# Softmax row sums on VectorE with one adding transfer, weight sums spread over the units, and a transposition moved behind the third scores

## The chip, the cores and the metric

One core of one Trainium2 chip runs the whole program. The metric is the device time of one execution in microseconds (us). Kernels are compared only within the same rounds. Names of engines: PE is TensorE, DVE is VectorE, ACT is ScalarE, POOL is GpSimd.

## The reference, cut to what matters

```python
# attention: q, k, v of shape (4, 8, 768, 64); six hash bits per row
mask = q_bucket[:, :, :, None] == k_bucket[:, :, None, :]
scores = scale * np.matmul(q, k.transpose(0, 1, 3, 2))
scores = np.where(mask, scores, -1000000000.0)
attn = np.exp(scores - np.max(scores, axis=-1, keepdims=True))
attn = attn / (np.sum(attn, axis=-1, keepdims=True) + 1e-09)
x = np.matmul(attn, v)                    # then (B,H,S,D) -> (B*S, H*D)
# feed-forward with a PReLU between two products
h = x @ w_in
g = np.maximum(h, 0.0) + alpha * np.minimum(h, 0.0)
return g @ w_out
```

## The kernel before

The attention stage works through 32 units: 16 pairs of heads, and for each the two halves of the queries. In a unit PE makes six score tiles in three groups of two ("first", "second" and "third scores"), ACT makes exponentials of them (`pt`), and one unit later PE multiplies these with v (`attend`) and with a matrix of ones (`totals`). Between these PE turns (transposes) q and k of the next pair in the even units and hashes them in the odd ones. DVE and GpSimd add six exponential tiles into one per unit. DVE also rounds one piece of the feed-forward's weights per unit (`weight_parts`, `weight_sum`), makes sums of rounded weights (`weight_group`; the products are of a kind with seven multiplications in place of eight, which needs such sums) and divides. The same kind of product needs four such sums (here differences) of the attention's result x for each batch; they are called the x sums, and GpSimd makes those of the first batch during the attention stage. After the attention stage come the products.

The loop of a unit, as it was:

```python
scores(u, 0)
add_first(u)                       # POOL: tile 0 + tile 1
...
if u > 0:
    add_last(u - 1)                # DVE: tiles 3 + 4, + 5, + POOL's sum
# (turn or hash of the first half), attend(u - 1, 0)
weight_parts(u)
scores(u, 1)
add_third(u)                       # POOL: + tile 2
weight_sum(u)
weight_group(u)                    # DVE: four sums at once, every 4th unit, later every 2nd
if more:
    if g == 0:
        turn(pi + 1, "k", 0)       # PSUM slot of the tag "mi"
        turn(pi + 1, "k", 1)       # the other one
    else:
        hash_bits(pi + 1, 1)
if u > 0:
    attend(u - 1, 1)
    totals(u - 1)                  # PSUM slot of the tag "mi"
...
scores(u, 2)
if u > 0:
    divide(u - 1)                  # DVE: its first step reads the totals
...
if u == HW:                        # HW = 16: w_in is rounded, the first batch's x long complete
    load_w(0); load_w(1); load_x(0); sums_x(0)     # the x sums: four subtractions on POOL
```

PSUM is the memory into which PE writes its results. The tag "mi" has two PSUM slots, taken in turn by both halves of a turn, by a hash and by the totals. Whoever takes a slot waits until the tile two takings back has been read.

## Time and profile before

| | before |
|---|---|
| median of 4 runs | 998.84 us (997.56 to 999.87) |
| span of the profiled run | 998.3 us |
| the add of 128x768, mean of 32, on DVE | 1667 ns |
| GpSimd: two adds per unit, mean of the first | 1939 ns |

```profile
PEclk9999999998999999999999999999999999999999
...
L676 DVE TENSOR_TENSOR accd<-accd,accp 128x768 f32<-128x768 f32 x32 | 53.4, 1667 | 3.3
```

These are two lines of the page: the granted clock of PE in 40 slices of the span, and a group of instructions with its busy time in us, the mean ns of one, and the idle time of its engine before it. The tenth slice (about 225 to 250 us) is the only one below 9. The mean of 1667 ns for the third add of DVE lies between the two durations that the prediction shows for it, 0.96 us with GpSimd idle and 2.39 us beside a GpSimd add.

### The profile page before, as it was taken

What the parts mean: (1) busy time and instruction counts of PE and PEld (TensorE: products, weight loads), DVE (VectorE), ACT (ScalarE), POOL (GpSimd) and SP (SyncE); (2) the same over time, 40 slices, a digit from 0 to 9 for tenths busy, and PEclk for the clock granted to TensorE, in tenths of its full rate; (3) what the DMA queues carried; (4) which work ended last, traced back from release to release, by engine and by line L of the source; (5) the groups of instructions that cost most, each with busy time, mean ns of one, the idle gap of its engine ahead of it and who ended that gap; (6) DMA issues with size and microseconds to landing.
All of it is one profiled execution on the core that took longest, in us unless ns stands there. A gap on an engine that the chain in (4) does not pass through costs nothing.

```text
span 998.3 us, 12489 instructions
## 1 busy us (share of the span) xinstructions
PE 963.2 (96%) x4741; PEld 594.0 (60%) x4741; DVE 605.8 (61%) x959; ACT 371.0 (37%) x669; POOL 158.5 (16%) x98
## 2 busy tenths in 40 slices
PE   6999999989999998999999999999999999999997
PEld 3444444434444443455788655888656888556886
DVE  3999999999999999766600366500467300665100
ACT  6777676665777664222100122100222000222000
POOL 2333333262333333000300000300000300000000
PEclk9999999998999999999999999999999999999999
DMA  7465756355444431463400133300224200231000
GB/s 199 126 182 143 237 154 179 107 164 157 143 143 143 127 111 53 200 259 110 137 22 22 58 111 99 123 22 21 71 88 155 68 22 22 84 111 37 22 22 24
DMA packets 93316, 106.81 MB, mean 107 GB/s; under 512 B 53296, under 2 KB 79936, under 8 KB 93248
## 3 DMA queue, kind: packets, MB, share of 16 engines
q1 hardware_dynamic: 91680, 105.54, 33.1%
q8 instruction: 39, 0.64, 0.3%
q10 hardware_dynamic: 1568, 0.39, 0.2%
q14 instruction: 29, 0.24, 0.1%
HBM read 78.65 MB, written 27.26 MB: 106 GB/s over the span
## 4 chain that ended last, share of the span: by engine, by line
PE 61%; DVE 35%; ACT 1%; issue 1%; DMA 1%; DVEq 0%; SPq 0%; ACTq 0%
PE z_2a L756 6%; PE z_1a L756 6%; PE z_0a L756 6%; DVE accd L676 5%; DVE accd L675 4%; DVE accd L674 4%; DVE wx L553 3%; PE z_1c L756 3%; PE z_0c L756 3%; PE z_2c L756 3%; DVE wr L577 2%; DVE wr L557 2%; PE f_2a L756 2%; PE f_3a L756 2%; PE f_7a L756 2%; PE f_6a L756 2%
## 5 line engine op out<-in xcount | busy, mean ns | idle before, releaser
L658 ACT ACTIVATE pt<-sc 128x768 f32<-128x768 f32 x192 | 149.9, 813 | 119.8 <-PE sc L653 119.8
L653 PE MATMUL sc<-qT,kT 64*128 64x384 f32 x768 | 157.5, 487 | 0.0
L686 PE MATMUL av<-pt,vn 128*64 128x385 f32 (+1 forms) x768 | 138.1, 495 | 0.0
L667 POOL TENSOR_TENSOR accp<-pt,pt 128x768 f32<-128x768 f32 x32 | 62.0, 1939 | 222.5 <-ACT pt L658 185.2
L686 PEld LDWEIGHTS av<-pt,vn 128*64 128x64 f32 x768 | 49.4, 136 | 72.6 <-issue 72.6
L732 POOL TENSOR_TENSOR x<-x,x 128x768 f32<-128x768 f32 x16 | 31.9, 2005 | 364.0 <-DMA x<-x_s 363.4
L810 DVE TENSOR_TENSOR g<-g,g 128x384 f32<-128x384 f32 x128 | 82.5, 665 | 2.2
L653 PEld LDWEIGHTS sc<-qT,kT 64*128 64x128 f32 x768 | 69.8, 190 | 15.3 <-issue 15.2
L653 PEld LDWEIGHTS <-kb 64*128 64x128 bf16 x384 | 24.4, 94 | 79.3 <-issue 62.7
L653 PE MATMUL sc<-qb,kb 64*128 64x384 bf16 x384 | 64.6, 329 | 5.6 <-ACT pt L658 5.6
L670 POOL TENSOR_TENSOR accp<-accp,pt 128x768 f32<-128x768 f32 x32 | 62.3, 1946 | 39.0 <-ACT pt L658 38.9
L756 PE MATMUL z_2a<-wo,g 128*128 128x256 f32 x256 | 58.0, 379 | 0.5 <-ACT z_2u L763 0.5
L756 PE MATMUL z_1a<-wo,g 128*128 128x256 f32 x256 | 57.9, 379 | 0.0
L756 PE MATMUL z_0a<-wo,g 128*128 128x256 f32 x256 | 57.9, 379 | 0.0
L676 DVE TENSOR_TENSOR accd<-accd,accp 128x768 f32<-128x768 f32 x32 | 53.4, 1667 | 3.3
L803 DVE SCALAR_TENSOR_TENSOR g<-h,alpha 128x384 f32<-128x384 f32 x32 | 22.1, 692 | 54.4 <-ACT h L795 54.4
L756 PEld LDWEIGHTS z_2a<-wo,g 128*128 128x128 f32 x256 | 48.6, 190 | 8.1 <-ACT z_2u L763 0.9
L756 PEld LDWEIGHTS z_0a<-wo,g 128*128 128x128 f32 x256 | 48.6, 190 | 7.5
L756 PEld LDWEIGHTS z_1a<-wo,g 128*128 128x128 f32 x256 | 48.6, 190 | 6.6
L675 DVE TENSOR_TENSOR accd<-accd,pt 128x768 f32<-128x768 f32 x32 | 43.7, 1364 | 3.3
L674 DVE TENSOR_TENSOR accd<-pt,pt 128x768 f32<-128x768 f32 x32 | 40.3, 1260 | 0.0
L639 ACT ACTIVATE qb<-hs,hb 32x384 bf16<-32x384 f32 x64 | 36.7, 574 | 2.2 <-PE hs L636 1.0
(217 smaller groups left out, 1477.1 us busy)
## 6 DMA issues: line engine op xcount, KB each, us to landing
wi<-w_in_s SPq DMA_DIRECT2D x32, 896.0 KB, 4.6
raw<-in_moe_w_in_dram SPq DMA_DIRECT2D x16, 512.0 KB, 4.1
raw<-in_moe_w_out_dram SPq DMA_DIRECT2D x16, 512.0 KB, 3.6
w_in_s<-wsi SPq DMA_DIRECT2D x16, 448.0 KB, 5.4
w_out_s<-wso SPq DMA_DIRECT2D x8, 896.0 KB, 4.4
wo<-w_out_s SPq DMA_DIRECT2D x8, 896.0 KB, 7.4
qn<-in_q_dram SPq DMA_DIRECT2D x32, 192.0 KB, 3.7
vn<-in_v_dram SPq DMA_DIRECT2D x16, 384.0 KB, 4.4
```

The lines of the kernel that those rows point to most:

```text
L639: do(ACT.activation(bits["q", pi][D * s : D * s + 32, cols], ps[r], AF.Sign, bias=hb[r]))
L653: do(PE.matmul(sc[:, s, :CW], what["k", pi][r, ks], what["q", pi][r, qs], start=first, stop=not first,))
L658: do(ACT.activation(pt[:, :, :CW], sc[:, :, :CW], AF.Exp, scale=SCALE / DOWN))
L667: do(POOL.tensor_tensor(accp[u], p(u, 0), p(u, 1), op=ALU.add))
L670: do(POOL.tensor_tensor(accp[u], accp[u], p(u, 2), op=ALU.add))
L674: do(DVE.tensor_tensor(accd[u], p(u, 3), p(u, 4), op=ALU.add))
L675: do(DVE.tensor_tensor(accd[u], accd[u], p(u, 5), op=ALU.add))
L676: do(DVE.tensor_tensor(accd[u], accd[u], accp[u], op=ALU.add))
L686: do(PE.matmul(av[u][D * s : D * s + D, :w], nat["v", pi][:, s, kc * D : (kc + 1) * D], prob[u, kc][:, s, :w], start=(kc == 0), stop=(kc = ...
L732: do(POOL.tensor_tensor(x_m[b, to], x_m[b, a], x_m[b, c], op=ALU.subtract))
L756: do(PE.matmul(self.ps[bank], self.left(left, k), self.right(right, k), start=start and k == 0, stop=k == self.nk - 1, skip_group_check=no ...
L810: do(DVE.tensor_tensor(g_m[to, i], g_m[x, i], g_m[y, i], op=op))
```

## The change

The intent: GpSimd's adds slow DVE down, so they go. DVE makes the first add itself, and the third tile is added by a transfer. The weight sums, four at once, made single units long for DVE; they are now queued and made one or two per unit. And the second turn (or hash) moves behind the third scores, so that PE has work while ACT makes exponentials.

```diff
+    def weight_sums(count):
+        while sums_due and (count or sums_due[0][0].__name__ == "store"):
+            ...                                    # [cut: one queued sum, or the store]
     def add_first(u):
-        do(POOL.tensor_tensor(accp[u], p(u, 0), p(u, 1), op=ALU.add))
+        do(DVE.tensor_tensor(accp[u], p(u, 0), p(u, 1), op=ALU.add))
     def add_third(u):
-        do(POOL.tensor_tensor(accp[u], accp[u], p(u, 2), op=ALU.add))
+        nc.gpsimd.dma_start(accp[u], p(u, 2), accum_op=ALU.add)
@@ the loop of a unit
         scores(u, 0)
-        add_first(u)
         if u > 0:
             add_last(u - 1)                        # now without the add of accp
+        add_first(u)
+        if u > 0:
+            add_total(u - 1)                       # the add of accp
@@
         weight_sum(u)
+        weight_sums(1 if u < HW else 2)
         weight_group(u)                            # now only queues
-        if more: ...                               # second turn or hash
         attend(u - 1, 1); totals(u - 1)
         scores(u, 2)
         divide(u - 1)
+        if more: ...                               # second turn or hash
-        if u == HW:
+        if u == HW + 2:
             load_w(0); load_w(1); load_x(0); sums_x(0)
```

More of the change, by code (lines that the diff above doesn't have):

```diff
@@ L584, in weight_sum @@
         ))
+    sums_due = []
     def weight_group(i):
@@ L597, in weight_group, with one, store @@
             return
-        for to, a, c in sums4:
+        def one(to, a, c):
             do(DVE.tensor_tensor(w[:, to], w[:, a], w[:, c], op=ALU.subtract))
-        if i < HW:
-            c, kk = divmod(n, 2)
-            for ii in range(4):
-                nc.sync.dma_start(w_in_s[4 * c + ii][:, :, kk], w[:, :, ii])
-        else:
-            nc.sync.dma_start(w_out_s[n], w)
+        def store():
+            if i < HW:
+                c, kk = divmod(n, 2)
+                for ii in range(4):
+                    nc.sync.dma_start(w_in_s[4 * c + ii][:, :, kk], w[:, :, ii])
+            else:
+                nc.sync.dma_start(w_out_s[n], w)
+        for x in sums4:
+            sums_due.append((one, x))
+        sums_due.append((store, ()))
+    def weight_sums(count):
+        while sums_due and (count or sums_due[0][0].__name__ == "store"):
+            fn, x = sums_due.pop(0)
+            count -= fn.__name__ == "one"
+            fn(*x)
     def turn(pi, name, half):
@@ L675, in add_last, with add_total @@
         do(DVE.tensor_tensor(accd[u], accd[u], p(u, 5), op=ALU.add))
+    def add_total(u):
         do(DVE.tensor_tensor(accd[u], accd[u], accp[u], op=ALU.add))
@@ L893, in fast_path @@
         weight_sum(u)
+        weight_sums(1 if u < HW else 2)
         weight_group(u)
-        if more:
-            if g == 0:
-                turn(pi + 1, "k", 0)
-                turn(pi + 1, "k", 1)
-            else:
-                hash_bits(pi + 1, 1)
         if u > 0:
@@ L908, in fast_path @@
             divide(u - 1)
+        if more:
+            if g == 0:
+                turn(pi + 1, "k", 0)
+                turn(pi + 1, "k", 1)
+            else:
+                hash_bits(pi + 1, 1)
         load_weight(u + 3)
-        if u == HW:
+        if u == HW + 2:
             load_w(0)
@@ L928, in fast_path @@
     add_last(last)
+    add_total(last)
     attend(last, 1)
@@ L932, in fast_path @@
     divide(last)
+    weight_sums(4)
     attn.close()
```

## The prediction

> **What bounds the kernel now.** I read the page's first two parts, then the table of stretches, then the timeline of the attention stage engine by engine, and only then the chain of waits.
>
> ```profile
> PE 963.2 (96%) x4741; PEld 594.0 (60%) x4741; DVE 605.8 (61%) x959; ACT 371.0 (37%) x669; POOL 158.5 (16%) x98
> ...
> 75.00:125.00 50.00, 48.75 (x330) 21.36 (x328) 47.79 (x70) 35.75 (x60) 16.76 (x9) 1.00 0.64 190
> 175.00:225.00 50.00, 46.18 (x308) 20.32 (x306) 47.96 (x61) 33.84 (x56) 23.44 (x12) 1.00 0.48 137
> 225.00:275.00 50.00, 48.49 (x306) 21.63 (x308) 47.65 (x72) 32.77 (x55) 14.79 (x8) 0.93 0.49 149
> 600.00:700.00 100.00, 100.00 (x419) 79.20 (x418) 31.80 (x51) 13.85 (x32) 7.89 (x4) 1.00 0.20 66
> ```
>
> The columns of the stretches are PE, weight loads, DVE, ACT, POOL, granted clock, DMA share, GB/s. After about 410 us (the matrix products) PE is full, and the change does not touch that. The attention stage, about 15 to 410 us, has 32 units (16 head pairs, two query halves); only there can time go. Both PE and DVE are over 95% busy in it, so the averages do not say which one binds.
>
> ```profile
> 130.53 0.87 PE L614 MATMUL tp_q<-ident,qn 128*128 128x128 f32 x6
> 130.58 0.95 DVE L674 TENSOR_TENSOR accd<-pt,pt 128x768 f32<-128x768 f32 x1
> 131.34 2.16 PE L686 MATMUL av<-pt,vn 128*64 128x384 f32 x12
> 132.43 1.85 POOL L667 TENSOR_TENSOR accp<-pt,pt 128x768 f32<-128x768 f32 x1 [6.98 <-ACT pt L658]
> 132.70 2.39 DVE L676 TENSOR_TENSOR accd<-accd,accp 128x768 f32<-128x768 f32 x1
> 135.14 0.87 PE L614 MATMUL tp_k<-ident,kn 128*128 128x128 f32 x6
> 135.72 1.71 DVE L553 TENSOR_SCALAR wx<-wx 128x512 uint32<-128x512 uint32 x1
> 137.93 0.82 PE L698 MATMUL sm<-accd,ones 128*64 128x384 f32 x4
> ...
> 142.36 0.51 PE L636 MATMUL hs<-kT,wh 128*32 128x384 f32 x1
> 142.67 1.50 ACT L658 ACTIVATE pt<-sc 128x768 f32<-128x768 f32 x2
> ```
>
> From the starts on PE, a unit is the same run of stages each time: first turn (or hash) 0.80, weighted sum of v 2.09, second scores 1.72, second turn 0.80, weighted sum 1.98, totals 0.75, then third scores and the next unit's first scores together 3.68. Sum 11.82 us. Most units are exactly that, whatever DVE does: PE has little left to give. It loses a little (1) where four score tiles follow one another (3.68 against 2 x 1.72 = 3.44: they wait for the exponentials, 0.24 per unit); (2) after a unit with weight sums, where the next turn waits for DVE to read the totals (a turn takes 1.61 in place of 0.80); (3) once, when GpSimd makes the x sums; (4) in the last two units, which have no turns, and where DVE is slower than PE (12.5 and 11.7 us).
>
> ```profile
> 210.37 8.39 POOL L732 TENSOR_TENSOR x<-x,x 128x768 f32<-128x768 f32 x4
> 212.68 2.19 DVE L557 SCALAR_TENSOR_TENSOR wr<-raw,wr 128x512 f32<-128x512 uint32 x1
> 224.74 0.96 DVE L676 TENSOR_TENSOR accd<-accd,accp 128x768 f32<-128x768 f32 x1
> 226.34 0.43 DVE L553 TENSOR_SCALAR wx<-wx 128x512 uint32<-128x512 uint32 x1
> ```
>
> This is the key to DVE: the same instructions with GpSimd idle. The add is 0.96 where it is 2.39 above, the shift 0.43 where it is 1.71.
>
> ```profile
> PE 61%; DVE 35%; ACT 1%; issue 1%; DMA 1%; DVEq 0%; SPq 0%; ACTq 0%
> ```
>
> The chain of waits runs through DVE for the whole attention stage. I take that with care: DVE never rests there, so a chain traced back through it finds no gap, yet PE's stages are as tight.
>
> **What the Trainium skill says.** "SBUF — State Buffer", section "Who interferes with whom": VectorE's second port pair is shared with GpSimd and locked for a whole instruction; a VectorE instruction with two SBUF inputs, or in a two-port mode, blocks against a GpSimd one that reads SBUF. The trace agrees (2.39 against 0.96; 1.71 against 0.43). "DMA: Bandwidth & Descriptors", section "SWDGE vs HWDGE vs iDMA": an accumulating transfer can only be issued from GpSimd, which writes its descriptors in software into SBUF. No transfer of that kind is in this trace. The same page, "Anatomy of one DMA — SWDGE (gpsimd) path", fits 2.0 us plus bytes over 436 GB/s, which is 2.9 us for 393 KB; the trace's plain 384 KB load of v takes 4.4, which I use. "Trainium Kernel Development and Optimization", section "Performance Expectations", warns that matmul busy time is a bad metric; hence the stage starts above instead of 96%.
>
> **The change part by part.**
>
> *DVE, per unit.* Removed: blocking by GpSimd, (2.39 - 0.96) + (1.71 - 0.43) = 2.7 us in the unit shown. Added: one 128x768 add, about 0.9 from start to start. Weight sums: before four at once (4 x 0.69 = 2.8 us every fourth unit, later 4 x 0.43 = 1.7 every second), now one (0.69) or two (0.86) per unit, the same total. Uncontended DVE per unit, start to start: adds 1.06 + 0.87 + 0.90 + 0.87 = 3.7; weight rounding 0.73 + 0.46 + 0.46 + 0.73 + 0.72 + 0.71 = 3.8; division 0.61 + 0.20 + 0.26 + 0.61 + 0.53 = 2.2; sums 0.7 to 0.9; together 10.4 to 10.6. That is about 1 us under PE's unit, so DVE's throughput stops binding.
>
> *PE, per unit.* The second turn or hash now stands between third and next first scores. It removes the 0.24 wait: 3 x 1.72 + 2 x 0.80 + 2.09 + 1.98 + 0.75 = 11.58 us.
>
> *The new wait.* The moved turn of k comes right after the totals in the small PSUM pair, so its second half takes the bank of the totals: it must wait until DVE has read them, the first step of the division. Let T be the end of third scores. The last exponential ends at T + 1.0 (142.36 shows hashes starting 1.7 after 140.6; ACT trails by 0.9). If the unit had a hash, ACT now does its three signs first (1.75), then the weight's absolute value and the square (1.4), and the next two exponentials (1.5): T + 5.6. DVE's first add needs both of them. After it: two adds 1.8, rounding 3.8, one sum 0.65, the transpose that reads the totals 0.57, so T + 12.4. PE wants the bank at T + 11.58 + 0.40 = T + 12.0. It stalls 0.5 us in every second unit, 0.75 with two sums.
>
> *Sum.* First half: a pair of units took 24.03 (48.04 us for four, first to fifth add of that kind), now 2 x 11.58 + 0.5 = 23.66; 8 pairs give 3.0. Second half: 24.39 now 23.91; 6 pairs give 2.9. Last units: traced the same way, the first product step after the totals starts about 29.4 us after unit 29's third scores, before 33.3 (409.58 - 376.32); 3.9 less. The x sums: four GpSimd adds of 2.1 us still block DVE, two units later, for about 6 us, and PE stalls as before: 0. The late sums of the last group (4 x 0.45) fall where PE has work queued: 0. Total 9.8 us: 999.6 - 9.8, about 990 us.
>
> **The rivals.**
> (a) *The adding transfer becomes the wait.* It can be issued at about T + 7.2 (its tile's exponential), and the adding of the totals needs it at about T + 17.7: 10.5 us of room. The v load takes 4.4; an accumulate must read its destination too, so I estimate 6 to 8 with descriptors. For: DMA is already half busy in this stage, and DVE's two-port steps may hold up descriptors. Against: the room. If it took 12 or 13 us, each unit would lose 1 to 3 us: 1020 to 1080.
> (b) *PE loses all stalls.* If ACT and DVE run slightly earlier than I work out, the 0.5 to 0.75 stall is gone: 8 x 0.87 + 6 x 1.23 + 3.9 = 18 us, 981; without the x sums' stall also, 976.
> (c) *DVE was the real bound, as the chain says.* Then a unit would go from 12.38 to about 10.6: 55 us saved, 945. PE's 11.82 in nearly every unit speaks against it.
> (d) *ACT's order costs more.* The exponentials now come 2 us later; if score tiles wait for them, PE gains nothing: about 1000.
>
> **Range and chances.** The gain is bounded by PE's tight stages at some 20 us, and the estimate sits in the middle; the transfer is the one unknown that could cost much. 990, with 979 to 1002 for 8 in 10. Faster by over 2% means under 979.6: only rival (b) in full, 0.11. Slower by over 2% (above 1019.6) only by rival (a): 0.07. Within: 0.82.
>
> **What would show it.** Right: the adds on DVE at 0.95 to 0.97 and the shift at 0.43 in all units but the one with x sums; the chain of waits moving from DVE to PE in the attention stage; units of 11.6 and 12.1 in turn on PE; a wait of the k turn on the transpose of the division; DVE waiting for the exponentials before the first add. Wrong: waits of the total add on a DMA (rival a), a DVE still long in its adds although GpSimd is idle (descriptors on the same ports), score tiles waiting on ACT (d), or no k-turn wait at all (b).

## The result, and the profile after

The changed kernel took 993.76 us in the median (4 runs, 993.52 to 995.21) against 998.84. The ratio is 0.9953, with a 95% interval from 0.9936 to 0.997: faster, but by less than 2%. Here and below a ratio is the mean time of one kernel's fast runs over that of the other's fast runs of the same rounds, so it is not quite the ratio of the medians.

The page of the changed kernel (its engine rows, PE's granted clock, the shares in the chain of waits, three groups of instructions, and the adding transfer with KB and median us from issue to landing):

```profile
PE 959.8 (97%) x4741; PEld 590.5 (60%) x4741; DVE 557.9 (56%) x991; ACT 373.1 (38%) x669; POOL 72.5 (7%) x66
PEclk9999999997999999999999999999999999999999
...
PE 77%; DVE 10%; ACT 8%; issue 3%; DMA 1%; SPq 0%; ACTq 0%; DVEq 0%
...
L685 POOL DMA_DIRECT2D accp<-pt x32 | 38.5, 1204 | 344.6 <-DVE accd L693 145.8
L682 DVE TENSOR_TENSOR accp<-pt,pt 128x768 f32<-128x768 f32 x32 | 30.7, 958 | 46.8 <-ACT pt L673 46.8
L693 DVE TENSOR_TENSOR accd<-accd,accp 128x768 f32<-128x768 f32 x32 | 30.5, 953 | 1.9 <-DMA accp<-pt 1.8
...
accp<-pt POOLq DMA_DIRECT2D x32, 384.0 KB, 4.8
```

DVE took on 32 more instructions and is busy 48 us less (557.9 for 605.8). The same add that took 1667 ns in the mean takes 953. The chain of waits went from DVE to PE, as foreseen. The transfer lands in 4.8 us and was waited for only 1.8 us in all. But the tenth slice of the clock went from 8 to 7: the x sums cost more than before.

One even unit of the changed kernel, cut to the lines that count (start, duration, engine, line of the kernel, operation, tiles; in brackets the idle time before and what ended it):

```profile
132.83 0.96 DVE L682 TENSOR_TENSOR accp<-pt,pt 128x768 f32<-128x768 f32 x1 [2.61 <-ACT pt L673]
133.71 0.95 DVE L693 TENSOR_TENSOR accd<-accd,accp 128x768 f32<-128x768 f32 x1
...
138.38 0.68 DVE L602 TENSOR_TENSOR wsi<-wsi 128x512 f32<-128x512 f32 x1
138.79 0.55 PE L629 MATMUL tp_k<-ident,kn 128*128 128x128 f32 x3
138.98 0.58 DVE L725 STREAM_TRANSPOSE st<-sm 128x384 f32<-128x384 f32 x1
139.61 0.55 PE L629 MATMUL tp_k<-ident,kn 128*128 128x128 f32 x3 [0.27 <-DVE st L725]
```

Read it from the bottom. The second half of the turn of k (139.61) waits for the transpose of the division (138.98 to 139.56), which empties the PSUM slot of the totals. DVE comes to that transpose late, because it waited 2.61 us for the exponentials before its first add (132.83), and because a weight sum (138.38, 0.68 us) stands directly ahead of it. PE's turn takes 1.30 us from its start to the next stage, in place of 0.80. It does so in the even units from 4 to 14. In unit 2, which comes before any weight sum is queued, there is no such wait: from its second scores to those of the next unit PE takes 11.57 us, and 12.07 in the even units from 4 to 14. That is a first sign, in the same trace, that the sum ahead of the transpose is what makes PE wait.

The accounting below takes, on PE in the timelines of both profiled runs, the start of the second scores of some units (and of the first product step after the totals of the last unit) and lists the time from one to the next.

| stretch of the attention stage | before | after | gain | predicted |
|---|---|---|---|---|
| start to unit 2 | 38.14 | 38.56 | -0.42 | 0 |
| units 2 to 16 | 167.75 | 164.97 | 2.78 | 3.0 |
| units 16 to 20 (the x sums) | 53.56 | 57.67 | -4.11 | 0 |
| units 20 to 30 | 120.92 | 118.68 | 2.24 | 2.9 |
| unit 30 to the first product step after the totals | 29.21 | 24.35 | 4.86 | 3.9 |
| sum | | | 5.35 | 9.8 |

The rest of the difference between the profiled spans (998.3 - 991.7 = 6.6 us) is 1.25 us in the products, where neither kernel was changed. There the profiled run of before ran slow for about 2 us behind a stop of 1.97 us at the check of the operands' magnitudes, and the profiled run of after, with the same stop, happened not to. Of the ten variants' profiled runs six did and four did not, so I take it as chance of a single execution.

What went wrong at the x sums, in the changed kernel's timeline:

```profile
230.57 2.87 DVE L553 TENSOR_SCALAR wx<-wx 128x512 uint32<-128x512 uint32 x1
230.85 8.40 POOL L749 TENSOR_TENSOR x<-x,x 128x768 f32<-128x768 f32 x4
233.47 1.92 DVE L556 TENSOR_SCALAR wr<-wx 128x512 uint32<-128x512 uint32 x1
235.42 2.17 DVE L557 SCALAR_TENSOR_TENSOR wr<-raw,wr 128x512 f32<-128x512 uint32 x1
237.63 2.17 DVE L577 SCALAR_TENSOR_TENSOR wr<-wx,wr 128x512 f32<-128x512 f32 x1
...
241.24 0.58 DVE L725 STREAM_TRANSPOSE st<-sm 128x384 f32<-128x384 f32 x1
241.87 0.90 PE L629 MATMUL tp_k<-ident,kn 128*128 128x128 f32 x3 [7.25 <-DVE st L725]
243.00 1.49 PE L668 MATMUL sc<-qT,kT 64*128 64x384 f32 x4
```

GpSimd's four subtractions run from 230.85 to 239.25. Four DVE steps of that time take 2.87, 1.92, 2.17 and 2.17 us, where they take 0.43, 0.43, 0.69 and 0.69 uncontended: 6.9 us more. All four lie ahead of the transpose that the turn of k needs, and PE stands for 7.25 us. Then the scores take 1.49 us for four matmuls that take 0.81 elsewhere. The table of stretches shows why, for the changed kernel (columns PE, weight loads, DVE, ACT, POOL, granted clock, DMA share, GB/s):

```profile
218.00:232.00 14.00, 14.00 (x96) 6.13 (x94) 11.67 (x20) 9.45 (x16) 3.10 (x3) 1.00 0.88 228
232.00:242.50 10.50, 3.25 (x22) 1.63 (x18) 10.23 (x11) 2.01 (x3) 7.10 (x4) 0.76 0.35 68
242.50:248.00 5.50, 5.50 (x26) 2.00 (x26) 3.86 (x6) 3.81 (x7) 0.00 (x0) 0.53 0.79 245
```

and for the kernel before, about its own x sums (first a line of PE's timeline, then the stretches):

```profile
225.84 1.55 PE L698 MATMUL sm<-accd,ones 128*64 128x384 f32 x4 [3.04 <-DVE accd L676]
...
214.00:226.00 12.00, 8.59 (x62) 3.15 (x61) 11.59 (x12) 7.67 (x13) 8.60 (x5) 0.96 0.38 123
226.00:232.50 6.50, 6.50 (x26) 3.08 (x27) 6.09 (x16) 2.50 (x4) 0.00 (x0) 0.54 0.34 94
```

Both kernels stop and then run at about half the clock (0.53 and 0.54). I add up from the stages' starts on PE by how much each took longer than elsewhere. Before: 0.43 ahead of a hash, 3.2 ahead of the totals (a stop of 3.04 us with nothing to do), and at the low clock 0.74 in the totals and 1.93 in the scores, 6.3 us together. After: 7.84 in the turn of k, and at the low clock 1.59 in the next first scores and 0.65 in the hash, 10.1 us together.

### The profile page after: what moved, and what is told of

Its sections match the earlier page's. It is cut to its first block, busy times and chain, and to the rows that moved or that the text cites. A ratio compares the mean times of both kernels' runs of the same rounds, so it can differ in the third digit from the quotient of the medians.

```text
span 991.7 us, 12469 instructions
## 1 busy us (share of the span) xinstructions
PE 959.8 (97%) x4741; PEld 590.5 (60%) x4741; DVE 557.9 (56%) x991; ACT 373.1 (38%) x669; POOL 72.5 (7%) x66
## 4 chain that ended last, share of the span: by engine, by line
PE 77%; DVE 10%; ACT 8%; issue 3%; DMA 1%; SPq 0%; ACTq 0%; DVEq 0%
PE sc L668 8%; PE av L703 7%; PE z_2a L773 6%; PE z_1a L773 6%; PE z_0a L773 6%; ACT pt L673 4%; PE z_1c L773 3%; PE z_2c L773 3%; PE z_0c L773 3%; PE f_0a L773 2%; PE f_2a L773 2%; PE f_7a L773 2%; PE f_3a L773 2%; PE f_6a L773 2%; PE f_5a L773 2%
## 5 line engine op out<-in xcount | busy, mean ns | idle before, releaser
L685 POOL DMA_DIRECT2D accp<-pt x32 | 38.5, 1204 | 344.6 <-DVE accd L693 145.8
L668 PEld LDWEIGHTS <-kb 64*128 64x128 bf16 x384 | 19.1, 93 | 66.5 <-issue 52.8
L682 DVE TENSOR_TENSOR accp<-pt,pt 128x768 f32<-128x768 f32 x32 | 30.7, 958 | 46.8 <-ACT pt L673 46.8
L820 DVE SCALAR_TENSOR_TENSOR g<-h,alpha 128x384 f32<-128x384 f32 x32 | 20.0, 625 | 50.9 <-ACT h L812 50.9
L690 DVE TENSOR_TENSOR accd<-accd,pt 128x768 f32<-128x768 f32 x32 | 30.7, 959 | 3.3
L693 DVE TENSOR_TENSOR accd<-accd,accp 128x768 f32<-128x768 f32 x32 | 30.5, 953 | 1.9 <-DMA accp<-pt 1.8
L689 DVE TENSOR_TENSOR accd<-pt,pt 128x768 f32<-128x768 f32 x32 | 30.4, 949 | 0.9 <-ACT pt L673 0.9
```

Source lines behind the costliest of these rows:

```text
L668: do(PE.matmul(sc[:, s, :CW], what["k", pi][r, ks], what["q", pi][r, qs], start=first, stop=not first,))
L682: do(DVE.tensor_tensor(accp[u], p(u, 0), p(u, 1), op=ALU.add))
L685: nc.gpsimd.dma_start(accp[u], p(u, 2), accum_op=ALU.add)
L689: do(DVE.tensor_tensor(accd[u], p(u, 3), p(u, 4), op=ALU.add))
L690: do(DVE.tensor_tensor(accd[u], accd[u], p(u, 5), op=ALU.add))
L693: do(DVE.tensor_tensor(accd[u], accd[u], accp[u], op=ALU.add))
```

## The experiments

Theory 1 (T1), formed from these traces: the three parts work against each other. The adds free DVE, but the moved turn makes PE wait directly on DVE's division, the weight sums of even units stand right ahead of that division, and the x sums hit the same place. Rivals: the transfer, the order of ACT's work or the clock holds the kernel back, or PE has nothing more to give. Every kernel below gave the right result.

### The second turn put back (a_noturn)

```diff
 # the changed kernel
         weight_group(u)
+        if more: ...          # second turn or hash, where it was before
         attend(u - 1, 1); totals(u - 1)
         scores(u, 2); divide(u - 1)
-        if more: ...
```

> The changed kernel with the second turn (or hash) put back behind the second scores; all else as changed. Theory 1 (TensorE is the bound, and the only new wait is the second half of the k turn on the bank that the division has still to read): the pair of units becomes 2 x 11.82 = 23.64 us, as in the changed kernel's first half (23.64) and 0.2 less than in its second (23.83), with no wait of a turn on the division; the one long stop at the x sums shrinks from 10 to 2 or 3 us, because the turn that needs the bank now comes 2.5 us later and the clock does not fall. About 985 us, ratio to the kernel before 0.986. Rival (the moved turn is worth its 0.24 us per unit): 7 us slower than the changed kernel, 1001. Rival (the x sums cost what they cost, wherever the turn stands): 993.

986.54 us, ratio 0.9873 [0.9857, 0.989]. Taking out the part that was to give PE work makes the kernel 7 us faster. Two units take 23.64 us, and no turn waits for the division. The part of the expectation about the x sums missed: PE still stopped for 2.25 us there, ahead of the totals, and the clock did fall (0.51 over the 3.5 us that follow), though the loss was only about 4 us.

```profile
246.57 1.55 PE L715 MATMUL sm<-accd,ones 128*64 128x384 f32 x4 [2.25 <-DVE accd L693]
```

The x sums stand in unit 18 here as in the changed kernel, so their move from unit 16 to 18 is not what made the stop longer.

### The weight sums put back, four at once (a_nosums)

```diff
-        weight_sums(1 if u < HW else 2)
         weight_group(u)
+        weight_sums(4)
```

> The changed kernel with a group's four weight sums done at once again, in the unit that ends the group (always a unit of odd number, with hashes). Theory 1: the k turn is in even units, which then have no sums; the transpose that frees the bank comes 0.65 to 0.9 us earlier there, so the 0.5 to 0.7 us wait of the k turn goes in all 14 or 15 pairs, and the bunch of 1.8 to 2.8 us in odd units meets no turn that needs the bank soon. Pairs of 23.16 us, about 8 us less than the changed kernel: 986. Rival (VectorE's bunches are what TensorE waits for, the reason for spreading them): slower than the changed kernel by 0.8 us in every pair with a group, 1003 or so.

987.11 us, 0.9877 [0.9861, 0.9894]. The units that make sums are odd ones, which hash; a hash has no second half that waits. So the turn of k takes 0.80 us again, and two units take 23.16 (2 x 11.58). The stop at the x sums stays: the turn of k takes 7.8 us in place of 0.80, and what follows 1.6 more. So it is the place of the sums that cost time, not their amount.

### The division ahead of the weight sums (a_divfirst)

```diff
         weight_sum(u)
-        weight_sums(1 if u < HW else 2)
-        weight_group(u)
         attend(u - 1, 1); totals(u - 1)
         scores(u, 2)
         divide(u - 1)
+        weight_sums(1 if u < HW else 2)
+        weight_group(u)
```

> The changed kernel with the spread weight sums moved behind the division on VectorE, nothing else. The same work on every engine. Theory 1: the bank is free 0.65 to 0.9 us sooner, the wait of the k turn goes, pairs of 23.16 us: 7 to 8 us less than the changed kernel, 986. The sums then lie in the 2 us in which VectorE waits for the exponentials. Rival (VectorE's total work binds, or the exponentials on ScalarE do): no difference, 993 to 995.

986.96 us, 0.9876 [0.9859, 0.9892]. Same work, same parts, only the order of two steps on DVE:

```profile
115.26 0.58 DVE L725 STREAM_TRANSPOSE st<-sm 128x384 f32<-128x384 f32 x1
...
115.61 0.87 PE L629 MATMUL tp_k<-ident,kn 128*128 128x128 f32 x6
...
117.49 0.68 DVE L602 TENSOR_TENSOR wsi<-wsi 128x512 f32<-128x512 f32 x1
```

In the timeline of this variant the six matmuls of the turn run through in 0.87 us (x6, with no bracket), the transpose is done before the second half needs its slot, and the weight sum comes after it. Two units take 23.16 us. The x sums still stop PE (the turn of k takes 7.85 us in place of 0.80, the scores behind it 2.95 in place of 1.72). So the wait is that of the slot, and the sum ahead of the transpose is its cause.

### The x sums on VectorE (a_xdve)

```diff
+        if HW + 4 <= u < HW + 8:
+            sums_x(0, (u - HW - 4,), DVE)   # one of the four per unit
         add_first(u)
@@
             load_x(0)
-            sums_x(0)                       # four on POOL
```

> The changed kernel with the four x sums of the first batch done by VectorE, one in each of units 20 to 23, just before the first two tiles are added, where VectorE waits for the exponentials anyway; GpSimd then computes nothing in the attention stage. Theory 1 (GpSimd blocks VectorE for the 8.4 us of these sums, which stops TensorE for 7.8 us and drops its clock for another 2.5): the 10 us stop goes, the clock stays at 1.00, 984. Rival (the stop comes from the loads of x and of the first weights that lie there too, or from the stores of the weights): the stop stays, 993. Rival (the sums cost VectorE as much): 2 to 4 us gained only, 990.

986.59 us, 0.9871 [0.9854, 0.9887], against 993.76 and 0.9953 with the sums on GpSimd. The stop is gone and the clock stays at 1.00 there: units 16 to 20 take 48.2 us for 57.7. The time still lies 2 to 3 us above what was expected. In the profiled run PE ran at half clock twice elsewhere, for 3.4 us each: from 20.3 us on, so that unit 2 was reached 1.2 us later than in the changed kernel, and behind the stop in the products. The ratios differ by 0.0082, 8.2 us, for a stop that I had added up to 10.1.

### One part alone: the adds (b_adds)

```diff
 # the kernel before
-        do(POOL.tensor_tensor(accp[u], p(u, 0), p(u, 1), op=ALU.add))
+        do(DVE.tensor_tensor(accp[u], p(u, 0), p(u, 1), op=ALU.add))
-        do(POOL.tensor_tensor(accp[u], accp[u], p(u, 2), op=ALU.add))
+        nc.gpsimd.dma_start(accp[u], p(u, 2), accum_op=ALU.add)
 # and add_total split from add_last, called behind add_first, as in the change
```

> The kernel before with only the adds changed: first two tiles on VectorE, third by the adding transfer, total add split off; weight sums in bunches, second turn and x sums where they were. Theory 1: TensorE is then at its old dense unit of 11.82 us everywhere, pairs of 23.64, VectorE has over a microsecond to spare per unit, and the x sums stop it for some 4 us as in the run with the turn put back: 986 or 987, so this part alone gives more than the whole change. Rival (each part of the change gives a share of the gain): between 994 and 998.

985.42 us, 0.9878 [0.9861, 0.9894]. One part of the change gives more than twice what all of it gives. Two units take 23.62 us throughout, 2 x 11.81: exactly the unit that the prediction found in before, now without the units that were longer. At the x sums, PE's timeline of this variant:

```profile
221.90 0.87 PE L700 MATMUL sm<-accd,ones 128*64 128x384 f32 x4 [1.80 <-DVE accd L678]
...
227.98 0.55 PE L614 MATMUL tp_q<-ident,qn 128*128 128x128 f32 x3 [1.05 <-DVE st L710]
```

PE stops twice, for 1.80 and 1.05 us, with five microseconds of work between, and the clock stays at 1.00. That the old order leaves DVE more time to catch up between these points is a reading of this timeline; no run tests it by itself.

### One part alone: the turn (b_turn)

```diff
 # the kernel before
         weight_group(u)
-        if more: ...          # second turn or hash
         attend(u - 1, 1); totals(u - 1)
         scores(u, 2); divide(u - 1)
+        if more: ...
```

> The kernel before with only the second turn moved behind the third scores. Theory 1: the 0.24 us per unit on TensorE can't be had, since GpSimd's adds keep VectorE without a pause at 12.0 us per unit, and the k turn now hangs on its division: 997 to 1001. Rival (TensorE's dense stages alone set the pace): 7 us less, 991.

1002.3 us, 1.004 [1.0025, 1.0055]: slower, slightly above the upper end of what was expected. The waits of this variant list 17.1 us in nine waits of the turn of k for the division's transpose, the longest 7.4; the turn takes about 2.5 us in every second even unit of the first half, 1.9 to 2.2 us in the second, and 8.8 at the x sums, in place of 0.80. With a DVE that is slowed by GpSimd, the turn is better left where it was.

### The third tile on VectorE, without a transfer (a_thirddve)

```diff
-        nc.gpsimd.dma_start(accp[u], p(u, 2), accum_op=ALU.add)
+        do(DVE.tensor_tensor(accp[u], accp[u], p(u, 2), op=ALU.add))
```

> The changed kernel with the third tile added on VectorE, no transfer. Theory 1: 0.9 us more on VectorE ahead of the division, so the k turn's wait goes from 0.5 to 0.7 up to 1.4 to 1.6 us in every even unit: 15 x 0.9 and some at the end, 1007 to 1010. Rival (VectorE has 1 us to spare per unit, so the transfer buys nothing): 993 to 995.

998.94 us, 1.0011 [0.9996, 1.0026]. The expectation was missed by 8 us. Two things had been left out. The turn of k takes only 0.65 us longer than with the transfer: the add takes 0.86 us from start to start, the step ahead of it is 0.11 shorter, and DVE's shift takes 0.43 us in every unit, where it took 0.52 in most even ones beside the issue of the transfer. And the x sums moved:

```profile
128.20 6.62 POOL L749 TENSOR_TENSOR x<-x,x 128x768 f32<-128x768 f32 x3 [47.24 <-DMA x<-x_s]
```

In this timeline GpSimd makes them at 128 us, not at 231. With no transfers ahead of them in GpSimd's instructions nothing held them back but their data, and there they cost PE about 4 us instead of 10. So the transfer is worth more than the 0.6% between the two ratios (1.0011 and 0.9953); how much, free of the second effect, was not measured.

### The transfer with less room (a_late)

```diff
-        nc.gpsimd.dma_start(accp[u], p(u, 2), accum_op=ALU.add)   # behind the second scores
+        nc.gpsimd.dma_start(accp[u], p(u, 5), accum_op=ALU.add)   # behind the third; DVE adds tiles 2, 3, 4
```

> The changed kernel with the transfer adding the sixth tile (exponential done 1.0 us after the third scores) in place of the third (some 4.4 us before them); VectorE adds tiles three to five instead. Same adds, same bytes, 5.4 us less room for the transfer. It takes 4.8 us in the changed kernel, so it would land some 5.9 us after the third scores, and the total add wants it at 6.1 to 6.6. Theory 1 (the transfer is hidden with room to spare): 993 to 996. Rival (the transfer's landing is what VectorE waits for, and a microsecond less room is a microsecond more per unit): 1010 or more.

1017.15 us against 999.25, 1.0181 [1.0157, 1.0206]. Theory 1's expectation fell here, and that of the rival held. In the view of the tile `accp` in this variant (DVE's idle time that the transfer ended, in us and times, and issue to landing):

```profile
  DMA accp<-pt: 45.8, 28
...
DMA to landing us min/median/max: 4.5/6.8/10.2
```

The same transfer, 384 KB, issued about 5.4 us later in the unit, lands in 6.8 us in the median where it took 4.8, and DVE waits for it 28 times. The fall is twofold: less room, and a slower transfer. That at this place it meets a store and several loads that are issued at the end of a unit would explain the second; no run took these away, so it stays open.

### All three parts, mended (best1), and with the turn put back (best3)

best1 is the changed kernel with the edits of a_divfirst and a_xdve together. best3 is the changed kernel with those of a_noturn and a_xdve.

> The changed kernel with both mends: weight sums behind the division, and the x sums on VectorE in units 20 to 23. Theory 1: the two gains add, since one is a wait in every even unit and the other one stop: pairs of 23.16 us without the stop, 979 to 980, ratio to the kernel before 0.980. Rival (with the sums moved into VectorE's pause, the x sums no longer fit there and bring waits): 983 or more.

> The changed kernel with the second turn put back and the x sums on VectorE: what the turn's move is worth once its wait on the division is mended, against the run with both mends (977.8). Theory 1: without the move, units of 11.82 in place of 11.58 us, less the 0.65 us that the move costs in the first unit: 29 x 0.24 - 0.65 = 6 us slower than that run, 983 to 984. Rival (the move itself is worth nothing): 978.

best1: 977.79 us, 0.9794 [0.9779, 0.9809], better than both kernels; against the kernel before it is about 2% faster, and whether it is over 2% the interval leaves unclear. best3: 982.11 us, 0.9832 [0.9818, 0.9845]. The engines in the page of best1 and, from its table of stretches, the time of the former stop:

```profile
PE 954.9 (98%) x4741; PEld 590.6 (61%) x4741; DVE 554.3 (57%) x995; ACT 371.6 (38%) x669; POOL 64.6 (7%) x62
```

```profile
225.00:250.00 25.00, 25.00 (x172) 10.98 (x168) 22.36 (x40) 18.65 (x32) 2.40 (x2) 1.00 0.92 248
```

PE is busy for all of 25 us at full clock, and most pairs of units take 23.16 us. The moved turn is worth 0.9832 - 0.9794, about 4 us, once nothing makes it wait; I had expected 6. The two profiled runs show where the rest went. From unit 2 to 30 PE takes 324.1 us in best1 and 329.9 in best3, 5.8 less, but best1 reaches unit 2 1.7 us later. In the first unit PE stops for 2.36 us in place of 1.30, since the turn is no longer there to fill the gap, and in this run it then ran at half clock for 3.4 us. Five of the eight profiled kernels with the moved turn did so there, and none of the four without.

Put together, with the adds done in all four:

| | sums four at once | sums spread |
|---|---|---|
| turn where it was | 0.9878 (b_adds, x sums in unit 16) | 0.9873 (a_noturn) |
| turn moved | 0.9877 (a_nosums) | 0.9953 (the change) |

Each of the two further parts alone adds next to nothing on top of the adds. Together they cost 0.75%, some 7 us. The adds and the transfer are the same in all four, and the turn is moved in both kernels of the lower row, so none of these explains it alone. "Next to nothing" is a sum for the turn: in the profiled runs of a_nosums and b_adds the moved turn gains 5.0 us in units 2 to 16 and 20 to 30, and loses 1.6 at the start and 4.4 in units 16 to 20, at the x sums.

## Why the prediction was right or wrong

**The class and the range held.** 993.76 us lies within 979 to 1002, and faster by less than 2% was the likeliest class. The gain was 5 us in place of 9.8. That the number lies so close to 990 is in part luck: the last units gave 1 us more than worked out, and 1.25 us of the profiled difference is chance in the products.

**The first half held.** Two units were to take 23.66 us and took 23.64; in the second half 23.91 was foreseen and 23.83 came. The wait that makes up the difference to 23.16 was named with its cause and its size: 0.5 and 0.75 us foreseen, 0.49 and 0.69 measured, on the transpose of the division. Its working holds as well: in the unit shown above, T (the end of third scores) is 127.2 us, the first add starts at T + 5.6, and the transpose ends at T + 12.3, where T + 5.6 and T + 12.4 were foreseen. The second half gave 2.24 where 2.9 had been worked out for six pairs of units; one of the six lies in the stretch of the x sums.

**The step that failed is the term of the x sums:** "four GpSimd adds of 2.1 us still block DVE, two units later, for about 6 us, and PE stalls as before: 0." The blocking was right (6.9 us). "As before" was wrong: it is -4.1 us. Before, PE met the late DVE at a hash (0.36 us) and then at the totals (3.04 us), with other work between. In the changed kernel the turn of k waits for DVE one step further on, with a wait of 0.5 to 0.7 us even undisturbed, so what DVE lost there came out on PE in full, 7.25 us in one piece, and the clock fell behind it. The prediction had found the new wait and the block, and never laid one over the other. a_xdve took away the block, and 8.2 us with it; a_noturn took away the wait, and the loss there went from 10.1 to about 4.

**Two smaller terms.** The first unit cost 0.42 us that were not foreseen: there the second turn had filled PE's wait for the first exponentials, and now comes after it. The last units gave 4.86 for 3.9. One reading of the shown lines is also off: PE is not over 95% busy in all of the attention stage (46.18 of 50 us from 175 to 225, 92%); nothing in the sum rests on it.

**The rivals.** (a) did not happen: the transfer landed in 4.8 us, where 6 to 8 had been estimated, and DVE waited 1.8 us for it in all. But a_late shows what hangs on the room: with 5.4 us less of it the same transfer costs 23 us against the changed kernel. (b), no stall at all, is not what the change does, but it is what its parts can do: 977.8 us in best1, 981 or 976 as its text has it. (c) fell with the pairs of units, which went from 24.03 only to 23.64. (d) fell too: DVE waits for exponentials 46.8 us in all before its first add, as the prediction said it would, but the score stages on PE are not longer.

## What to carry to other kernels

When a step of the busiest engine is moved, ask which buffer it takes and who has to empty that buffer; the move can turn a slack of microseconds into a wait that any delay of the other engine passes on in full. Put spread-out work where it does not stand ahead of such an emptying, rather than evenly. And before trusting "as before" for a rare event, lay it over the new waits: the cost of a block depends on what comes next, and not on the block alone.

## What the Trainium skill lacked or had wrong

- "TensorE: Matmul & The Clock Gate", section "What's actually happening", gives the half rate after at least one idle window of about 3.4 us, in a free-running window. A stop of 7.25 us was followed by a granted 0.53, which agrees. But shorter stops cost clock too. In the kernel before a stop of 3.04 us was followed by 0.54, and the clock fell 2.3 us after PE had gone idle; in a_noturn a stop of 2.25 us was followed by 0.51 over 3.5 us. The stop of 1.97 us at the check of the magnitudes is the same in all twelve profiled runs, and the clock fell to half within 2 us of its end in seven of them and not in five. Two stops of 1.80 and 1.05 us apart from each other (b_adds) cost none. In all these cases the half clock lasted 3.4, 6.8 or 10.2 us.
- "SBUF — State Buffer", section "A bandwidth-pool intuition that's wrong (but worth ruling out)", warns of about 620 growing to about 3100 ns where GpSimd can't write descriptors beside VectorE. Here the issue of the adding transfer stayed at 1200 ns in the median (1329 at most) beside a busy VectorE, and VectorE's shift beside it took 0.52 us for 0.43 (it is 0.43 in every unit of a_thirddve, which has no such transfer).
- "DMA: Bandwidth & Descriptors", section "SWDGE vs HWDGE vs iDMA", says that accumulating goes through GpSimd's queue, but has no cost for it. Measured: 384 KB within SBUF, 4.8 us to landing in the median (4.3 to 10.8), 6.8 when issued at the end of a unit, and 1.2 us of GpSimd for each.
- No page gives what several GpSimd instructions in a row do to a row of VectorE instructions: here each VectorE step took the length of about one GpSimd step (1.92 to 2.87 us against 8.40 / 4 = 2.1), whatever its own length.
